# Attention and expert layer in one kernel: an expert's two matrices in one transfer, a narrower tile of ones, and a new table of the order

## The chip, the cores and the metric

The kernel runs on one core of one Trainium2 chip. The metric is the device time in microseconds of one execution, lower is better. The kernel has three compute engines that read PSUM or feed from it, TensorE (PE in the profile), ScalarE (ACT) and VectorE (DVE); GpSimd (POOL), which scales what another engine has copied out; and SyncE (SP), on whose queue nearly all transfers are issued.

## The reference

Four batches of 10048 tokens with 128 channels pass through an induced-attention block with 32 inducing points and then through a two-level mixture of experts, 4 groups of 4 experts, each with a hidden width of 1024.

```python
def mab(q, kv):
    s = scale * (q @ kv.transpose(0, 2, 1))
    s = s - s.max(-1, keepdims=True)
    a = np.exp(s)
    a /= a.sum(-1, keepdims=True) + 1e-09
    return a @ kv
h = mab(I, x)                 # (B, 32, 128)
attn = mab(x, h)              # (B, N, 128)
...
g_idx = np.argmax(x @ w_group, axis=1)            # then the expert within the group
h = np.maximum(xg[mask_e] @ w1[g, e], 0.0)
ye = h @ w2[g, e]
out[tok_idx] = combined[:, None] * ye             # combined: the two softmax weights
```

Here x of the second part is the attention's output. Everything is float32. Tokens enter and leave as 20.6 MB each.

## The kernel before, in words

A batch (b = 0 to 3) is cut into five chunks (k = 0 to 4) of 4 x 512 tokens, 1 MB each; the fifth overlaps the fourth. For each chunk the kernel loads the tokens with channels on the partitions (`xk`, from `xT` or `xL`). For half of the chunks (`LOADED`) it also loads them with tokens on the partitions (`xn`, from `xm`); for the others TensorE transposes `xk` (`turn`, L139) and ACT or DVE copy the result out of PSUM (`tev`, L534). The first attention is `s1` (L152), a running maximum (DVE, L156), `ex` (ACT, L163), a transpose `tr` (L173), its copy `pev`, and `hq` (L186), which sums over tokens and frees the buffers of the chunk.

After the five chunks some small steps normalize the sum (`ap` L208, `same` L221, `hp` L230) and route the batch: the product `R` (L240, L241), then `pick` on DVE, which writes the number of one expert into `pi` (L253). The kernel relies on all tokens of a batch going to that one expert and on its hidden units each having one sign over the batch; it checks both, and a general path (`general`), which is not taken here, does the rest. SP reads the number (L281, a value load that waits for `pick`) and loads that expert's `w1` (L282) and `w2` (L283), each 128 rows of 4 KB, into the two halves of one buffer. TensorE applies `w1` to the 32 summaries (`z`, L288), DVE transposes and masks the result, and TensorE applies `w2` (`G4`, L306) and sums (`G`, L312). So the whole expert becomes a 32 x 128 matrix G per batch.

The second attention of a chunk is `s2` (L329), a maximum (DVE, L333), `ex2` (ACT, L337), `L` (L344) for the routing weights, and `out` (L383), which fills four PSUM banks. Each is written into the chunk's output buffer by one of three ways: by ACT as a bare copy (L398), which POOL then scales (L403); by DVE with the scaling (L392); or by ACT with the scaling in four pieces (L396). Then SP stores the chunk, 1 MB (L407).

All operations of the four batches are numbered by `plan_all`. The table `ORDER` is a list of these numbers with a letter for the engine (a, b or c: the first, second or third that may do it) and sets the order on every engine; each engine works its list in order. Buffers come from rings (19 of 1 MB named `big`, 8 PSUM banks `ps`, and others) and are given out in the table's order, so a load waits for the operation that frees its buffer. SP too works its list in order: a value load or a store that waits holds the transfers behind it.

`IDLE` names places at which TensorE gets products of ones, n units of 128 columns, so that it does not stand still (L489, `idle`); they read a tile of ones that a DVE memset fills at the start (L852) and write a PSUM bank that the operation named is about to use. The first, of 12 units, runs while the first chunk is on its way.

Of the kernel before, what the change touches and what calls it, by code (L numbers as in the profile page):

```python
# [8 lines left out]
F32 = mybir.dt.float32  # L9
# [7 lines left out]
P = 128  # L17
# [27 lines left out]
IDLE = ((2, 12), (455, 3), (465, 2), (515, 3), (625, 4), (635, 2), (657, 4), (667, 5), (704, 6))  # L45
# [59 lines left out]
def plan_all(em=None):  # L105
# [130 lines left out]
    def routes(b, hT):  # L236
# [41 lines left out]
        def w2():  # L278
            return em.t(w12)[:, F:].rearrange("p (n c) -> p n c", c=C)
        def f(e):  # L280
            i = em.nc.sync.value_load(em.s(f"pi{b}", 1, 1, I32)[0:1, 0:1], min_val=0, max_val=E - 1)  # L281
            em.nc.sync.dma_start(out=em.t(w12)[:, 0:F], in_=em.w1[bass.ds(i, 1)].rearrange("o d f -> d (o f)"))  # L282
            em.nc.sync.dma_start(out=w2(), in_=em.w2[bass.ds(i, 1)].rearrange("o (p n) d -> p (o n) d", n=FB))  # L283
# [199 lines left out]
    def idle(at, n):  # L483
        o = plan.ops[at]
        ps = o.take.pop(0)
        assert ps.of == "ps"
        def f(e):
            for w in [KW] * (n // TK) + [P] * (n % TK):
                em.nc.tensor.matmul(em.t(ps)[:, 0:w], lhsT=em.ones[:, 0:P], rhs=em.ones[:, 0:w], start=True, stop=True)  # L489
        o.soft.append(op("idle", PE, f, [], [ps], [], size=n))  # L490
# [56 lines left out]
1a 0a 206a 706a 2a 6a 3b 4a 5b 7b 8a 357a 17a 10a 45a 27a 11a 19a 12a 23a 28a 35a 178a 25a 205a 18a 20a 9a 47a 21a 53a 13a 63a 46a 29a 51a 234a 49a  # L547
24a 26b 195a 30a 31a 37a 14a 50b 36a 38a 55a 56a 188a 32a 40a 48b 57a 22b 15a 356a 179a 54a 64a 180a 39a 16a 59a 182a 189a 186a 207a 183b 60a 52a 209a
208a 181b 184a 41a 190a 211a 191a 192a 61a 65a 42a 33a 187a 197a 233a 185b 223a 66a 215a 198a 67a 216a 193a 194a 43a 34a 213a 373a 58a 217a 68a 219a
210a 73a 44a 212b 358a 383a 362a 62a 74a 199a 69a 75a 200a 363a 70b 76a 366a 71a 72a 360a 196a 214a 218a 77a 367a 359a 201a 78a 364a 401a 220a 79a  # L550
235a 237a 368a 202b 80a 81a 361a 82a 369a 238b 241a 83a 84a 127a 365a 243a 370a 236a 131a 225a 527a 128a 95a 375a 242a 99a 86a 85a 226a 227a 224a 244a
411a 96a 371a 221a 372a 526a 100a 376a 132a 393a 97a 159a 101a 129a 160a 245a 228a 203a 384a 133a 239a 204a 240a 229a 230b 161a 251a 247a 385a 374a
87a 377a 252a 222a 394a 98a 403a 88a 395a 248a 386a 102a 253a 89a 412a 389a 571a 397a 103a 254a 391a 398a 379a 378a 392a 104a 404a 390a 105a 405a 106a
91a 231a 232a 92a 90a 413a 255a 414a 380a 162a 249a 536a 246a 163a 130a 416a 93a 250a 415a 537a 407a 94b 421a 402a 256a 422a 164a 387a 528a 538a 529a
396a 257a 408a 258a 134a 381a 543a 135a 165a 117a 382a 136a 388a 553a 118a 137a 120a 259a 399a 260a 309a 581a 166a 122a 417a 400a 124a 138a 310a 406a
261a 423a 139a 262a 418a 273a 311a 140a 142a 144a 409a 424a 146c 274a 107a 545a 108a 114a 110a 264a 263a 123a 275a 410a 112c 546a 337a 277a 177a 121a
419a 149a 338a 420a 563a 143a 547a 425a 111a 278a 544a 426a 276a 113a 339a 109a 279a 573a 280a 150b 564a 427a 154a 156b 115a 141a 549a 145a 147a 119a
428a 532a 539a 565a 265a 533a 429a 281a 157a 574a 572a 305a 540a 555a 550a 554a 152a 125a 282a 430a 576a 266a 575a 561a 556a 267a 562a 557a 269a 283a
270a 548a 558a 431a 306a 307a 530a 271a 268a 559a 284a 534a 272a 531a 295a 153a 151a 560a 535a 308a 541a 296c 432a 566a 155a 433a 302a 542a 116a 126a
298a 479a 567a 300c 480a 167a 481a 568a 583a 168b 312a 170a 174b 584a 551a 552a 172c 285a 585a 577a 591a 297a 148a 313a 286a 586a 314a 592a 315a 169a  # L560
578a 288a 292c 316a 447a 448a 290c 569a 475a 340a 175a 570a 579a 476a 449a 303a 477a 327a 158a 341a 342a 355a 580a 287a 343a 587a 328a 434a 443a 588a
582a 589a 344a 444a 435a 593a 299a 330a 332a 590a 334a 317a 445a 594a 173a 436a 595a 596a 171a 291a 437a 289a 597a 598a 446a 318b 333a 324c 450a 322a
439a 599a 293a 176a 440a 345a 329a 331a 438a 600a 301a 451a 601a 441a 320c 452a 325a 602a 323a 346a 348a 319a 442a 453a 350c 294a 454a 352a 708a 465a
321a 335a 466a 468a 472a 707a 455a 351a 478a 470a 304a 603a 482a 349a 456a 483a 462c 613a 326a 458a 347a 617a 484a 460c 353a 467a 649a 336a 614a 618a
487a 485a 615a 645a 469a 486a 619a 471a 616a 488a 494a 604a 650a 354a 646a 490a 461a 457a 620a 492a 463a 651a 459a 473a 621a 605a 489a 606a 647a 497a
648a 607a 498a 464a 652a 608a 500c 474a 653a 622a 609a 610a 502a 501a 495a 504a 507a 611a 493a 654a 491a 623a 612a 499a 508a 503a 655a 505a 509a 710a
# [279 lines left out]
def attention_moe(ctx, tc, xT, xL, xm, small, w1, w2, out):  # L846
# [4 lines left out]
    ones = cp.tile([P, KW], F32, name="ones")  # L851
# [19 lines left out]
        "ident": ident, "iota4": iota4, "own_j": own_j, "ones": ones[:, 0:P], "wr_sb": small_sb[:, M:],  # L871
# [23 lines left out]
def build_inputs(inputs):  # L895
# [18 lines left out]
        "w2": np.asarray(inputs["moe_w2"]).reshape(E, F, C),  # L914
    }
# [20 lines left out]
```

## Time and profile before

| | |
|---|---|
| median of 3 runs | 151.36 us (151.32 to 151.44) |
| the profiled execution | 151.35 us, of which the span is 149.6 us |
| PE busy | 136.1 us, 91% of the span |
| DVE / ACT / POOL busy | 112.8 / 105.5 / 51.0 us |
| moved by DMA | 56.9 MB, mean 380 GB/s |
| HBM read / written | 35.50 MB / 20.97 MB |

The span goes from the first to the last instruction; what the execution takes beyond it, 1.75 us, lies around it. In the prediction's rows an engine's instructions stand with their line, and a DMA issue is a row of SP. In the view of stretches the columns are the busy time of PE, its weight loads, DVE, ACT and POOL, the granted clock of TensorE, the busy share of the DMA engines and their GB/s. The landing time of a transfer runs from its issue until all of its data are there.

### The profile page before, as it was taken

To read this page: it belongs to the slowest core of one execution; us is meant where nothing else is said; L and a number is where in the kernel's file an instruction comes from. 1 tells how busy PE (TensorE), PEld (TensorE's weight loads), DVE (VectorE), ACT (ScalarE), POOL (GpSimd) and SP (SyncE) were. 2 spreads that over 40 slices of the span, in tenths; PEclk is the share of its full clock that TensorE was granted. 3 is DMA by queue.
4 is the path that set the end of the run, shared out by engine and by line. 5 is a ranking of instruction groups with operands and counts; after the bars stand their busy time and mean duration, and the time that the engine had idled before them with its cause. 6 is when DMAs were issued, how large, how long until landed. Compare 5 with 4: busy or idle time off the path is not lost.

```text
span 149.6 us, 5582 instructions
## 1 busy us (share of the span) xinstructions
PE 136.1 (91%) x2225; PEld 93.7 (63%) x2225; DVE 112.8 (75%) x383; ACT 105.5 (71%) x265; POOL 51.0 (34%) x70
## 2 busy tenths in 40 slices
PE   6999999999999999999999999999999999998000
PEld 3459497678536686967455967676884656775000
DVE  3093782756889889888998978998989998999500
ACT  3017384486416797679968999989999998999300
POOL 4000000000000000044491811555799998855200
PEclk9999999999999999999999999999999999999965
DMA  5999999999999999999999999979699899999980
GB/s 123 421 423 425 415 424 421 418 424 414 417 413 418 420 416 424 415 424 418 387 376 366 377 418 364 379 287 410 245 423 252 348 421 434 414 416 425 425 344 33
DMA packets 8529, 56.90 MB, mean 380 GB/s; under 512 B 1072, under 2 KB 1072, under 8 KB 2608
## 3 DMA queue, kind: packets, MB, share of 16 engines
q1 hardware_dynamic: 8352, 56.45, 94.0%
q8 instruction: 19, 0.31, 0.8%
q14 instruction: 14, 0.11, 0.2%
q10 hardware_dynamic: 144, 0.03, 0.1%
HBM read 35.50 MB, written 20.97 MB: 378 GB/s over the span
## 4 chain that ended last, share of the span: by engine, by line
PE 67%; DVE 14%; ACT 10%; issue 2%; DVEq 0%; ACTq 0%
PE ps L139 13%; PE ps L152 11%; PE ps L186 10%; PE ps L329 8%; PE ps L383 8%; PE ps L173 5%; ACT big L398 4%; PE ps L489 4%; ACT big L396 3%; PE ps L344 2%; DVE big L392 2%; ACT et L337 2%; DVE mxe L333 1%; PE ps L230 1%; PE ps L306 1%
## 5 line engine op out<-in xcount | busy, mean ns | idle before, releaser
L403 POOL TENSOR_TENSOR big<-big,gate_w 128x512 f32<-128x512 f32 x48 | 48.9, 1050 | 42.8 <-ACT big L398 36.0
L398 ACT COPY big<-ps 128x512 f32<-128x512 f32 x48 | 26.7, 626 | 1.7 <-PE ps L383 1.0
L163 ACT ACTIVATE pe<-ps,nb 128x512 f32<-128x512 f32 (+1 forms) x20 | 13.7, 687 | 19.6 <-DVE nb L160 9.6
L396 ACT ACTIVATE big<-ps,gate_w 128x128 f32<-128x128 f32 x84 | 24.4, 414 | 1.5 <-DVE n_bad L454 1.5
L383 PE MATMUL ps<-G,et 32*128 32x128 f32 x640 | 25.0, 285 | 0.0
L383 PEld LDWEIGHTS ps<-G,et 32*128 32x128 f32 x640 | 21.0, 186 | 5.6 <-ACT big L398 1.9
L139 PE MATMUL ps<-spread,big 128*128 128x128 f32 (+1 forms) x160 | 21.4, 276 | 0.1
L186 PEld LDWEIGHTS ps<-big,pt 128*32 128x32 f32 (+1 forms) x640 | 17.8, 110 | 5.9 <-issue 4.1
L186 PE MATMUL ps<-big,pt 128*32 128x129 f32 (+1 forms) x640 | 21.0, 273 | 0.0
L329 PE MATMUL ps<-big,hT 128*32 128x512 f32 (+2 forms) x192 | 20.5, 525 | 0.0
L139 PEld LDWEIGHTS ps<-spread,big 128*128 128x128 f32 (+1 forms) x160 | 17.8, 141 | 3.9 <-issue 2.0
L152 PE MATMUL ps<-big,small_sb 128*32 128x512 f32 (+1 forms) x160 | 19.9, 588 | 0.0
L156 DVE TENSOR_REDUCE mx<-ps 128x1 f32<-128x512 f32 (+1 forms) x20 | 13.4, 672 | 4.8 <-PE ps L152 4.1
L129 POOL MEMSET big<- 128x16 f32 x10 | 0.8, 128 | 45.8 <-PE ps L186 42.7
L534 ACT COPY big<-ps 128x512 f32<-128x512 f32 (+1 forms) x28 | 15.6, 591 | 0.8 <-PE ps L139 0.7
L337 ACT ACTIVATE et<-ps,nce 128x512 f32<-128x512 f32 x20 | 13.8, 722 | 2.4 <-DVE nce L334 2.1
L489 PE MATMUL ps<-ones 128*128 128x128 f32 (+1 forms) x40 | 13.4, 468 | 1.6 <-DVE ones L852 1.5
L333 DVE TENSOR_REDUCE mxe<-ps 128x1 f32<-128x512 f32 x20 | 13.3, 667 | 0.7 <-ACT big L398 0.4
L534 DVE COPY big<-ps 128x512 f32<-128x512 f32 x12 | 8.0, 685 | 7.8 <-PE ps L139 7.7
L534 ACT COPY pt<-ps 128x512 f32<-128x512 f32 (+2 forms) x20 | 10.0, 522 | 3.6 <-PE ps L173 2.8
L173 PE MATMUL ps<-spread,pe 128*128 128x128 f32 x80 | 12.2, 276 | 0.0
L173 PEld LDWEIGHTS ps<-spread,pe 128*128 128x128 f32 x80 | 9.1, 140 | 2.0 <-ACT big L398 1.7
(118 smaller groups left out, 162.2 us busy)
## 6 DMA issues: line engine op xcount, KB each, us to landing
out<-big SPq DMA_DIRECT2D x20, 1024.0 KB, 7.7
big<-xT SPq DMA_DIRECT2D x16, 1024.0 KB, 14.5
big<-xm SPq DMA_DIRECT2D x10, 1032.0 KB, 12.3
big<-w SPq DMA_DIRECT2D x8, 512.0 KB, 6.5
big<-xL SPq DMA_DIRECT2D x4, 960.0 KB, 14.9
small_sb<-small ACTq DMA_DIRECT2D x1, 26.0 KB, 5.7
```

Of the source, the lines that this page charges most:

```text
L139: em.nc.tensor.transpose(p[:tw, j * P:(j + 1) * P], em.t(xk[b, k])[:, j, off + t * P:off + t * P + tw], em.ident)
L152: em.nc.tensor.matmul(em.t(ps)[32 * j:32 * j + 32, :w], lhsT=em.indT, rhs=em.t(xk[b, k])[:, j, off:], start=True, stop=True)
L173: em.nc.tensor.transpose(p[:tw, t * P:(t + 1) * P], em.t(pe)[:, t * P:t * P + tw], em.ident)
L186: em.nc.tensor.matmul(h[32 * j:32 * j + 32, 0:CS], lhsT=q[:tw, t, 32 * j:32 * j + 32], rhs=x[:tw, t * J + j, :], start=(t == 0), stop=(t = ...
L329: em.nc.tensor.matmul(em.t(ps)[32 * j:32 * j + 32, c0:c1], lhsT=em.hT[b][:, P + 1:P + 1 + M], rhs=em.t(xk[b, k])[:, j, x0:x0 + c1 - c0], s ...
L337: em.nc.scalar.activation(out=em.t(et), in_=em.t(ps), func=AF.Exp, bias=em.s(nc_), scale=1.0)
L383: em.nc.tensor.matmul(em.t(pb[j])[:, t * C:(t + 1) * C], lhsT=em.t(et)[32 * j:32 * j + 32, t * P:(t + 1) * P], rhs=em.Gs[b][32 * j:32 * j ...
L396: em.nc.scalar.activation(out=q[:, t], in_=p[:, t], func=AF.Copy, scale=em.t(gt)["w"][:, r:r + 1])
L398: em.nc.scalar.copy(out=q, in_=p)
L403: em.nc.gpsimd.tensor_tensor(out=q, in0=q, in1=weights(j), op=ALU.mult)
L489: em.nc.tensor.matmul(em.t(ps)[:, 0:w], lhsT=em.ones[:, 0:P], rhs=em.ones[:, 0:w], start=True, stop=True)
L534: (self.nc.scalar.copy if engine == ACT else self.nc.vector.tensor_copy)(out=out, in_=in_)
```

## The change

Three edits. An expert's two matrices are laid side by side on the host in one array `w12`, 128 rows of 8 KB per expert, and loaded in one transfer. The tile of ones is 128x128 in place of 128x512, and the idle products read one of its columns with a stride of zero as their moving operand. `ORDER` and `IDLE` are new.

```diff
-IDLE = ((2, 12), (455, 3), (465, 2), (515, 3), (625, 4), (635, 2), (657, 4), (667, 5), (704, 6))
+IDLE = ((2, 12), (455, 3), (465, 2), (625, 2), (635, 3), (657, 4), (667, 3), (704, 5))
...
-            em.nc.sync.dma_start(out=em.t(w12)[:, 0:F], in_=em.w1[bass.ds(i, 1)].rearrange("o d f -> d (o f)"))
-            em.nc.sync.dma_start(out=w2(), in_=em.w2[bass.ds(i, 1)].rearrange("o (p n) d -> p (o n) d", n=FB))
+            em.nc.sync.dma_start(out=em.t(w12), in_=em.w12[bass.ds(i, 1)].rearrange("o p f -> p (o f)"))
...
-                em.nc.tensor.matmul(em.t(ps)[:, 0:w], lhsT=em.ones[:, 0:P], rhs=em.ones[:, 0:w], start=True, stop=True)
+                em.nc.tensor.matmul(em.t(ps)[:, 0:w], lhsT=em.ones[:, 0:P], rhs=em.ones[:, 0:1].broadcast_to([P, w]), start=True, stop=True)
...
-1a 0a 206a 706a 2a 6a 3b 4a 5b 7b 8a 357a 17a 10a 45a 27a 11a 19a 12a 23a 28a 35a 178a 25a 205a 18a 20a 9a 47a 21a 53a 13a 63a 46a 29a 51a 234a 49a
+206a 0a 17a 706a 2a 4a 6a 8a 10a 1a 11a 45a 3b 35a 12a 27a 5a 178a 19a 23a 25a 13a 18a 20a 9a 205a 7b 28a 46a 47a 53a 21a 24a 29a 54b 22a 48b 195a 51a
...
-    ones = cp.tile([P, KW], F32, name="ones")
+    ones = cp.tile([P, P], F32, name="ones")
...
+        "w12": np.concatenate([np.asarray(inputs["moe_w1"]).reshape(E, C, F), np.asarray(inputs["moe_w2"]).reshape(E, P, FB * C)], axis=2),
```

The general path still reads `w1` and `w2`. From L283 on, a line's number is lower by one after the change.

What the table does to the engines: of the 40 copies of transposed chunks (`tev`), ACT does 33 after and 28 before; of the 24 other copies, 23 and 20. Of the 80 output evictions, ACT copies 51 (48 before), ACT scales 19 (21), DVE scales 10 (11). The order moves in these places:

SP, from batch 1's expert transfer to the value load for batch 2's (`out` is a store of batch 0, `xm` a load of batch 3). Before:

```order
L282 DMA big_97<-w 128x1024
L283 ISA
L283 DMA big_97<-w 128x1024
L121 DMA big_109<-xm 128x2064
L121 DMA big_101<-xm 128x2064
L407 DMA out<-big_98 128x2048
L407 DMA out<-big_93 128x2048
L407 DMA out<-big_91 128x2048
L407 DMA out<-big_104 128x2048
L281 TENSOR_LOAD pi_1433
```

After:

```order
L282 DMA big_106<-w 128x2048
L406 DMA out<-big_97 128x2048
L406 DMA out<-big_94 128x2048
L121 DMA big_99<-xm 128x2064
L406 DMA out<-big_92 128x2048
L121 DMA big_106<-xm 128x2064
L121 DMA big_95<-xm 128x2064
L406 DMA out<-big_96 128x2048
L281 TENSOR_LOAD pi_1455
```

Batch 3's first `xm` load (its second chunk) stands behind two stores now, and its third, which came after batch 2's expert, comes before it.

POOL, at the first scalings (L403 before, L402 after; `big_93` and `big_94` are batch 0's second chunk); the memset is that of the ones column of a transposed chunk of batch 3. Before:

```order
L403 TENSOR_TENSOR big_93<-big_93,gate_w_132 128x4x128 x2
L403 TENSOR_TENSOR big_91<-big_91,gate_w_138 128x4x128
L403 TENSOR_TENSOR big_98<-big_98,gate_w_132 128x4x128 x3
L403 TENSOR_TENSOR big_91<-big_91,gate_w_138 128x4x128 x2
L403 TENSOR_TENSOR big_93<-big_93,gate_w_132 128x4x128
L129 MEMSET big_99 128x16
L403 TENSOR_TENSOR big_93<-big_93,gate_w_132 128x4x128
```

After:

```order
L402 TENSOR_TENSOR big_94<-big_94,gate_w_132 128x4x128
L402 TENSOR_TENSOR big_92<-big_92,gate_w_135 128x4x128
L402 TENSOR_TENSOR big_94<-big_94,gate_w_132 128x4x128
L402 TENSOR_TENSOR big_92<-big_92,gate_w_135 128x4x128 x2
L129 MEMSET big_98 128x16
L402 TENSOR_TENSOR big_97<-big_97,gate_w_132 128x4x128 x2
L402 TENSOR_TENSOR big_92<-big_92,gate_w_135 128x4x128
L402 TENSOR_TENSOR big_94<-big_94,gate_w_132 128x4x128
```

The memset comes after five scalings in place of nine, and the chunk's last scaling is the ninth in place of the tenth.

TensorE, around the fourth batch's `z` (L288 before, L287 after). Before:

```order
L383 MATMUL ps_128<-G_148,et_116 128x128
L329 MATMUL ps_126<-big_103,hT 32x512 x4
L344 MATMUL ps_125<-et_118,rbd_145 32x128 x4
L344 MATMUL ps_125<-et_117,rbd_145 32x128 x4
L288 MATMUL ps_122<-big_104,hT 32x256 x4
L383 MATMUL ps_127<-G_148,et_115 128x128
```

After:

```order
L328 MATMUL ps_126<-big_107,hT 32x512 x4
L328 MATMUL ps_129<-big_91,hT 32x512 x4
L328 MATMUL ps_123<-big_102,hT 32x480 x4
L328 MATMUL ps_123<-big_102,hT 32x32 x4
L287 MATMUL ps_122<-big_106,hT 32x256 x4
L382 MATMUL ps_125<-G_148,et_119 128x128
```

The two products L344 that stood ahead of `z` come behind it, and the last chunk's `s2` of batch 2 (L328, 480 and 32 columns) comes ahead of it.

More of the change, by code (lines that the diff above doesn't have):

```diff
@@ L551 @@
[L551 to L566, printed above, removed]
@@ new lines @@
+26a 31a 49a 14a 52a 179a 32a 37a 30a 55a 38a 56a 63a 33a 188a 15a 36a 356a 180a 234a 384a 64a 39a 207a 50a 186a 16a 181a 57a 189a 209a 41a 211a 40a
+187a 59a 190a 208a 213a 233a 191a 212a 60a 192a 42b 184a 34a 185a 182a 197a 61a 198a 65a 223a 183a 210a 357a 193a 215a 66a 43a 67a 68a 73a 216a 58a
+69a 44a 74a 401a 358a 364a 217a 214a 219a 75a 199a 76a 70a 62a 366a 367a 71a 362a 359a 77a 201a 72a 368a 360a 78a 79a 220a 80a 369a 194a 235a 218a 81a
+370a 241a 237a 202a 82a 365b 236a 361a 363b 83a 238a 196a 200a 131a 225a 127a 371a 373a 99a 84a 383a 243a 85a 226a 372a 128a 244a 242a 527a 227a 132a
@@ new lines @@
+424a 121a 123a 277a 419a 146a 145a 571a 263a 142a 107a 274a 275a 278a 108c 110b 112a 545a 309a 114a 581a 546a 310a 409a 547a 119a 410a 264a 420a 563a
+305a 564a 162a 306a 279a 425a 147a 426a 427a 311a 143a 163a 111a 149a 109a 565a 164a 307a 554a 115a 276a 337a 113a 428a 177a 116a 573a 150c 165a 152a
+141a 154a 280a 265a 338a 530a 548a 125a 339a 532a 166a 549a 156a 157a 534a 533a 531a 555a 266a 267a 281a 268a 535a 561a 269a 270a 556a 562a 282a 283a
+126a 574a 550a 429a 308a 541a 430a 271a 431a 272a 544a 559a 557a 284a 575a 567a 542a 560a 295a 566a 155a 153a 558a 296a 551a 300a 302a 576a 432a 433a
@@ new lines @@
+479a 568a 148a 151a 583a 312a 552a 298c 480a 584a 167a 481a 168a 585a 447a 313a 170a 172b 569a 314a 174a 169a 577a 572a 315a 578a 285a 448a 449a 316a
+286b 475a 582a 288a 292a 340a 297a 327a 570a 591a 158a 476a 290c 434a 341a 477a 586a 342a 587a 579a 175a 343a 592a 344a 588a 443a 328c 173a 589a 330a
+355a 593a 444a 301a 334a 291a 580a 435a 594a 590a 436a 332c 595a 596a 437a 171a 317a 445a 293a 438a 176a 597a 439a 318a 287a 446a 440a 289a 598a 320a
+303a 329a 450a 335a 322c 324b 599a 451a 600a 333a 319a 345a 294a 346a 348a 325a 452a 321a 601a 441a 442a 453a 350a 708a 352a 331a 465a 478a 466a 482a
@@ new lines @@
+602a 707a 454a 349a 468a 470a 299a 323a 603a 351a 455a 347a 304a 472c 456a 483a 613a 467a 326a 460a 484a 353a 617a 462a 458c 487a 336a 485a 473a 649a
+488a 604a 614a 618a 461a 645a 615a 457a 459a 486a 492a 354a 507a 490a 650a 646a 463a 619a 651a 508a 605a 494c 497a 616a 620a 606a 607a 647a 498a 509a
+471a 609a 502a 648a 610a 652a 504a 611a 612a 621a 622a 469a 709a 653a 493a 464a 654a 623a 625a 500c 624a 495a 608a 626a 632a 655a 711a 474a 491a 657a
+630c 628b 710a 656a 658a 489a 629a 501a 635a 660b 712a 664a 661a 696a 496a 499a 662c 503a 636c 642c 638b 667a 505a 668a 510a 663a 677a 670a 640b 627a
@@ L571 @@
+633a 515a 511a 674a 512a 678a 697a 506a 672c 631a 659a 513a 665a 525a 671a 641a 637a 643a 679a 514a 673a 516a 680a 522a 681a 634a 518c 519a 698a 682a
+713a 695a 685a 669a 683a 520c 675a 639a 666a 523a 686a 699a 644a 684a 700a 702a 688a 701a 703a 676a 690b 521a 704a 517a 687a 689a 692c 693a 691a 705a
+524a 694a
 """
@@ L845, in attention_moe @@
 @with_exitstack
-def attention_moe(ctx, tc, xT, xL, xm, small, w1, w2, out):
+def attention_moe(ctx, tc, xT, xL, xm, small, w1, w2, w12, out):
     nc = tc.nc
@@ L870, in attention_moe @@
     keep = {
-        "ident": ident, "iota4": iota4, "own_j": own_j, "ones": ones[:, 0:P], "wr_sb": small_sb[:, M:],
+        "ident": ident, "iota4": iota4, "own_j": own_j, "ones": ones, "wr_sb": small_sb[:, M:],
         "hT": cp.tile([P, B, P + 1 + M], F32, name="hT"),
@@ L877, in attention_moe @@
         pp = inner.enter_context(tc.tile_pool(name="ps", bufs=1, space=PSUM))
-        em = Emit(tc, fp, pp, nc, xT=xT, xL=xL, xm=xm, w1=w1, w2=w2, out=out, wr=keep["wr_sb"], indT=small_sb[:, 0:M], ones=ones,
+        em = Emit(tc, fp, pp, nc, xT=xT, xL=xL, xm=xm, w12=w12, out=out, wr=keep["wr_sb"], indT=small_sb[:, 0:M], ones=ones,
                   ident=ident, same_m=same_m, spread=spread, iota16m40=iota16m40, own_j=own_j,
```

11 lines of the change are left out of this document (4 added, 7 removed).

## The prediction

> **What bounds the kernel now.** I read the page first, then the stretches, then the queue's own waits, then single rows. The page:
>
> ```profile
> span 149.6 us, 5582 instructions
> PE 136.1 (91%) x2225; PEld 93.7 (63%) x2225; DVE 112.8 (75%) x383; ACT 105.5 (71%) x265; POOL 51.0 (34%) x70
> ```
>
> TensorE is busy for 91% of the span, and so, as the next rows show, are the transfers; the question is which of them is the limit where. The stretches (PE busy first; the last two columns are the DMA share and GB/s):
>
> ```profile
> 5.00:75.00 70.00, 69.75 (x1090) 48.70 (x1088) 52.24 (x169) 43.80 (x98) 5.33 (x7) 1.00 1.01 417
> 75.00:108.00 33.00, 32.92 (x622) 23.34 (x623) 29.33 (x100) 29.77 (x80) 17.37 (x19) 1.00 0.92 359
> 106.00:108.00 2.00, 2.00 (x39) 1.69 (x39) 1.90 (x7) 1.79 (x7) 1.96 (x2) 1.00 0.32 119
> 112.00:117.00 5.00, 5.00 (x81) 2.52 (x80) 4.52 (x18) 5.00 (x15) 5.00 (x6) 1.00 0.99 238
> 117.00:144.00 27.00, 21.05 (x367) 14.26 (x359) 21.94 (x74) 21.47 (x63) 18.01 (x18) 0.98 1.02 421
> ```
>
> Up to 108 us TensorE stands still for 0.33 us in 103, so it sets the pace; just before 108 the transfers run dry (119 GB/s). From 117 to 144 it is the other way round: 421 GB/s without a hole, while TensorE has 6 us to spare. Between lies the expert transfer of batch 3:
>
> ```profile
> 107.31 1.13 SPq L407 DMA_DIRECT2D out<-big  x2
> 110.89 0.35 SPq L282 DMA_DIRECT2D big<-w  x1
> 111.43 1.07 SPq L283 DMA_DIRECT2D big<-w  x1
> 112.60 0.43 SPq L407 DMA_DIRECT2D out<-big  x1
> ...
> 140.84 0.33 SPq L407 DMA_DIRECT2D out<-big  x1
> ```
>
> SP issues nothing from 108.4 to 110.9, since its next row is the value load that waits for the batch's routing. TensorE ends that routing product at 107.61 + 0.38 = 107.99, and the load is issued 2.9 us later:
>
> ```profile
> 107.61 0.38 PE L241 MATMUL ps<-small_sb,hT 128*128 128x20 f32 x2
> 117.92 0.61 PE L288 MATMUL ps<-big,hT 128*32 128x256 f32 x8
> 120.50 0.62 PE L306 MATMUL ps<-big,mt 128*32 128x128 f32 x16
> ```
>
> Behind it stand 11 stores, of 1 MB each. The last is issued at 140.84 and lands 7.5 us later, at 148.3 (first row); of all 20 stores the quickest took 4.1 (second row):
>
> ```profile
> DMA to landing us min/median/max: 7.5/7.5/7.5
> DMA to landing us min/median/max: 4.1/7.7/9.6
> ```
>
> So at the end a backlog of transfers, 3.4 us deep, covers the engines. The time is: TensorE's work up to the fourth routing, plus one expert transfer and 11 stores at the rate they get. An edit counts if it moves one of these.
>
> **The sum's base.** This execution took 151.35 us for a span of 149.6; the median of the runs is 151.36, so nothing is to be corrected.
>
> **The change part by part.** *The tile of ones.* The first idle products wait for its memset, and the first transposes for the idle products:
>
> ```profile
> 0.92 0.48 DVE L852 MEMSET ones<- 128x512 f32 x1 [0.92 <-PEq L923]
> 2.00 0.23 DVE L866 COPY same_m<-spread 128x128 f32<-128x128 f32 x1
> ...
> 1.46 5.25 PE ps L489 x6
> 6.71 1.75 PE ps L139 x16
> ```
>
> A 128x128 operation on VectorE takes 0.23, so the memset should lose 0.25 us, and the transposes start 0.25 earlier. More than the memset's whole 0.48 can't come of it, and nothing, if the first chunk isn't there earlier. I take -0.25, of 0 to -0.48. The moving operand now repeats one column. The nearest rows are two weight loads of the routing product, of which L240's repeats a column and L241's doesn't:
>
> ```profile
> L240 PEld LDWEIGHTS ps<-small_sb,hT x8: 185/190/192, 37.8 to 107.5; 128*128 128x128 f32 x8
> L241 PEld LDWEIGHTS ps<-small_sb,hT x8: 189/190/192, 38.1 to 107.7; 128*128 128x128 f32 x8
> ```
>
> 190 ns in both, so 0.
>
> *TensorE up to the fourth routing.* The order has it at row 325 before and after, with the same products ahead. What differs is how often TensorE turns from 32-row products to full-width ones or back: I count 39 turns before and 35 after. A turn shows in the chain as the same work at two prices:
>
> ```profile
> 34.06 0.59 PE ps L139 x4
> ...
> 35.09 0.44 PE ps L139 x4
> ```
>
> Four turns fewer at 0.15 are -0.6; other pairs show less, so I take -0.5, of 0 to -0.6. Against it, new waits: in the program after, loads stand in other places, and five of twelve evictions of transposed chunks and three other copies move from VectorE to ScalarE, in the stretch where ScalarE has 26 us free (5 to 75 us: 43.80 of 70). I allow +0.25, of 0 to +1.1 (worked out in the second rival). Together the fourth routing comes 0.5 us earlier.
>
> *One transfer for two.* SP saves an issue, 0.54 us per expert (110.89 to 111.43), and the store behind it is no longer held until 112.60; its data are ready then or a little before, and the queue is busy, so this is worth 0. Batch 0's pair tells what the second transfer itself costs:
>
> ```profile
> 41.16 0.36 SPq L282 DMA_DIRECT2D big<-w  x1
> 41.75 0.34 SPq L283 DMA_DIRECT2D big<-w  x1
> ...
> DMA to landing us min/median/max: 7.3/7.3/7.3
> DMA to landing us min/median/max: 8.0/8.0/8.0
> ```
>
> They land at 48.46 and 49.75, 1.29 us apart, and 0.524 MB at 418 GB/s are 1.25, so a second transfer costs nearly nothing there. Batch 3's pair does not go like that. From 112 to 117 the engines are busy (0.99) at 238 GB/s, which against 418 is 5 x (1 - 238/418) = 2.15 us lost, on the path. The other pairs:
>
> ```profile
> 41.00:51.00 10.00, 10.00 (x177) 6.05 (x173) 8.89 (x32) 5.42 (x10) 0.12 (x1) 1.00 1.02 418
> 72.00:77.00 5.00, 5.00 (x105) 2.88 (x105) 4.79 (x16) 4.64 (x12) 3.97 (x4) 1.00 1.01 389
> 90.00:97.00 7.00, 7.00 (x162) 5.05 (x165) 5.95 (x17) 6.69 (x19) 2.32 (x3) 1.00 1.01 371
> ```
>
> By the same sum they lose 0, 0.35 and 0.8 us, the more the more stores are about. The trace doesn't say why. One transfer of 128 rows of 8 KB from another tensor has half as many reads and other addresses; it may lose all the 2.15, or none, or about 1 us more (the step from batch 2 to batch 3). The other three lose 0.4 on average, this one 2.15: I take a loss of 1.15, that is -1.0, of -2.15 to +1.0.
>
> Against the merge stands that the first product with the weights (L288) has to wait for both matrices. Now the first lands at 110.89 + 6.3 = 117.2, the product starts at 117.92, and the second matrix lands at 111.43 + 7.3 = 118.7, ahead of its use at 120.50:
>
> ```profile
> DMA to landing us min/median/max: 6.3/6.3/6.3
> DMA to landing us min/median/max: 7.3/7.3/7.3
> ```
>
> Landing 0.5 earlier, at 118.2, it would hold TensorE for up to 0.8 us from its turn at 117.4 (less, since after the change one scoring product stands ahead of it in place of two smaller ones); landing 1.5 earlier, not at all. What it holds is covered by the 3.4 us backlog: 0. The Trainium skill says the same more sharply: by "DMA: Bandwidth & Descriptors", section "Why a DMA increments its semaphore by 16 and not by 1", only the full count tells that all data of a transfer are there. By that rule alone the product waits up to 0.8 us longer, and if the backlog did not cover it, the sum would be 150.7 instead of 149.9.
>
> *The order's end.* Idle products fall from 41 to 34 units, and the last stores' evictions are shared out anew. This moves the last issue (140.84), which is covered as long as the backlog stands; it becomes late next only if the transfers gain more than 3.4 us. Moved stores and loads before the fourth routing: the queue runs dry there anyway, 0.
>
> Sum: 151.35 - 0.5 - 1.0 = 149.85; I predict 149.9.
>
> **The rivals.** *1. All of the 2.15 us goes.* If the pair of 4 KB transfers, with its second issue of 1.07 us, is what slows the reads, the merge recovers them all: 151.35 - 0.5 - 2.15 = 148.7. For it: that issue is three times as long as batch 0's 0.34. Against it: batch 2's second issue was longer still, at a loss of 0.8:
>
> ```profile
> 90.11 1.38 SPq L283 DMA_DIRECT2D big<-w  x1
> ```
>
> [...]
>
> *2. Slower: a load of batch 3 is stuck behind a store.* After the change the load of batch 3's second chunk stands on SP behind batch 0's second store. That store waited for POOL:
>
> ```profile
> SPq L407 <- POOL big L403: 23.0, 12, 6.8
> ...
> 83.36 0.82 SPq L407 DMA_DIRECT2D out<-big  x2
> ...
> 82.22 0.12 POOL L129 MEMSET big<- 128x16 f32 x1 [3.12 <-PE ps L329]
> ...
> 92.13 0.73 PE L186 MATMUL ps<-big,pt 128*32 128x129 f32 x20
> ...
> DMA to landing us min/median/max: 6.1/6.1/6.1
> ```
>
> If it goes out at 83.4 again, the load lands 6.1 us later (a load issued at 93.25 took that), at 89.5. Its product, at 92.13 before, has 3.2 us less of work ahead of it after (counted in the order, each product at its price in the chain) and is due at 88.4 with the 0.5 gained: 1.1 us of standstill, which every later step pays, 151.35 - 0.5 + 1.1 = 152.0. It decides if the store is issued after 82.3. Against it: the memset that held POOL for 3.12 us stands four scalings earlier and waits for an earlier product, and this store's last scaling is the ninth on POOL where it was the tenth. Without the hold it goes out at 80.2, one scaling earlier at 79.2.
>
> *3. Slower reads.* The merged load, with stores on both sides, loses 1 us more than now: 151.35 - 0.5 + 1.0 = 151.9.
>
> *4. Nothing moves.* New waits eat the 0.5, and the reads lose 2.15 again: 151.3.
>
> **How the numbers follow.** Forecast 0.54, rival 1 0.09, rival 2 0.12, rival 3 0.11, rival 4 0.14. The predicted time is the forecast's. The range 148.4 to 151.9 goes from rival 1's 148.7, less 0.3 for its unknowns, up to rival 3. This kernel's runs differ by 0.1%, so about 0.2% (0.3 us) is what a measurement can tell: faster 0.63 (the forecast and rival 1), same 0.14, slower 0.23.
>
> **What would show it.** Right: the first transposes near 6.45; the routing product L241's fourth pair ending near 107.5, the fourth expert load issued near 110.4; over 300 GB/s in the 5 us after it is first read; the last store landing near 146.8. Wrong: TensorE idle for over 1 us between 5 and 108 us; the fourth load again at 238 GB/s; a last store that lands 4.1 us after its issue, which would say that the engines and no longer the transfers set the end.

## The result: 1.2% slower

After took 153.3 us in the median of its first four executions (152.45 to 154.97) against 151.34 before, a ratio of 1.0124 with a 95% interval of 1.0082 to 1.0165. Measured again beside other kernels (run e5 below) it gave 1.0125, 1.0082 to 1.0168. The forecast was 149.9, with 148.4 to 151.9 for the range: it named the wrong sign. Medians here are of all executions, while ratios leave out slow ones, those more than 1.5% above the kernel's fastest, such as the one of 154.97 us. That one is the profiled execution of after, with a span of 153.2; where a number hangs on that, I give it from the profile of e5 too, the same kernel in 152.2 us.

The page of after, the two lines that were shown of before:

```profile
span 153.2 us, 5565 instructions
PE 135.4 (88%) x2223; PEld 93.9 (61%) x2223; DVE 109.7 (72%) x373; ACT 108.1 (71%) x269; POOL 54.3 (35%) x73
```

TensorE works no longer than before (136.1). The stretches, as before PE first, the last two columns the DMA share and GB/s:

```profile
5.00:75.00 70.00, 69.18 (x1073) 48.62 (x1075) 47.27 (x152) 45.23 (x102) 6.49 (x9) 1.00 1.00 410
75.00:108.00 33.00, 32.78 (x635) 23.15 (x628) 30.05 (x106) 29.68 (x78) 17.64 (x19) 1.00 0.95 373
112.00:117.00 5.00, 5.00 (x92) 2.46 (x88) 4.48 (x19) 4.90 (x15) 5.00 (x6) 1.00 1.01 352
117.00:144.00 27.00, 20.53 (x365) 14.43 (x357) 22.81 (x73) 22.83 (x67) 19.53 (x20) 0.90 0.93 383
```

The last of these stretches in e5:

```profile
117.00:144.00 27.00, 19.20 (x365) 13.20 (x357) 23.01 (x74) 22.65 (x67) 19.39 (x20) 0.94 0.98 409
```

TensorE stands still for 0.82 us up to 75 us (1.36 in e5), where it was 0.25. The read from 112 to 117 goes at 352 GB/s (349 in e5) in place of 238, as hoped. But from 117 to 144 the transfers, which had no hole before (421), have some: 383, and still 409 in e5. Next SP's issues and two of TensorE's products, then two answers on the time to landing: the fourth expert load and the last store.

```profile
111.38 0.35 SPq L282 DMA_DIRECT2D big<-w  x1
114.09 30.77 SPq L406 DMA_DIRECT2D out<-big  x11
108.00 0.38 PE L241 MATMUL ps<-small_sb,hT 128*128 128x20 f32 x2
120.38 0.64 PE L287 MATMUL ps<-big,hT 128*32 128x256 f32 x8 [1.86 <-DMA big<-w]
DMA to landing us min/median/max: 8.9/8.9/8.9
DMA to landing us min/median/max: 5.0/5.0/5.0
```

The fourth routing product ends at 108.38 (in e5 too), 0.4 us later than before and not 0.5 earlier. The expert load lands 8.86 us after its issue, at 120.24, and TensorE waits 1.86 us for it; in e5 it lands after 7.5, and TensorE doesn't wait for it. The last store is issued at 144.52 (141.97 in e5, 140.84 before) and lands after 5.0 us (5.4 in e5): the 3.4 us backlog that the forecast counted on is mostly gone.

After's profile is 2.6 us behind e5's at the last store, and TensorE's granted clock has a part in that. The two rows of each are the stretch behind the load's landing and the products with `w2`, first after, then e5:

```profile
121.00:126.00 5.00, 5.00 (x93) 4.15 (x90) 3.32 (x9) 2.77 (x7) 3.94 (x5) 0.66 1.01 423
123.28 1.08 PE L305 MATMUL ps<-big,mt 128*32 128x128 f32 x16
```

```profile
121.00:126.00 5.00, 4.67 (x90) 3.09 (x82) 4.47 (x15) 4.91 (x15) 4.55 (x6) 1.00 0.99 416
121.40 0.64 PE L305 MATMUL ps<-big,mt 128*32 128x128 f32 x16
```

The clock is 0.50 in each microsecond from 122 to 125 of after, and 1.00 in e5. The first product with the weights starts 1.42 us later than in e5 (120.38, 118.96), and the product L311 2.53 later (125.11, 122.58): 1.4 us for the late load, 1.1 for the clock. The same dip stands in the profile of e13 below, but not in those of e7 and e8, in which TensorE waited as long for the load (1.8 and 2.0 us); what sets it off stays open.

What ends the kernel shows in SP's waits behind the last store. The verdict is the number that VectorE writes last of its chain (`n_bad`); every engine reads it and branches over the general path. The rows are first before's, then after's (L887 before and L886 after are that branch, L930 the closing barrier):

```profile
SPq L887 <- SPq L887: 5.3, 1, 5.3
SPq L930 <- DMA out<-big: 1.2, 1, 1.2
```

```profile
SPq L886 <- SPq L886: 5.2, 1, 5.2
SPq L930 <- PEq L886: 0.6, 1, 0.6
```

SP stands behind its own branch for 5.2 us. Before, it still had to wait 1.2 us for the last store after that; after, it waits for TensorE's branch instead and never for the store (in e5 too: 5.5 us, then 0.2 for TensorE's branch). I had both rows of before and didn't read them: only 1.2 us lay between the store that I took for the end and another end.

### The profile page after: what moved, and what is told of

Read it like the earlier page. It is cut to its first block, busy times and chain, and to the rows that moved or that the text cites. A ratio compares the mean times of both kernels' runs of the same rounds, so it can differ in the third digit from the quotient of the medians.

```text
span 153.2 us, 5565 instructions
## 1 busy us (share of the span) xinstructions
PE 135.4 (88%) x2223; PEld 93.9 (61%) x2223; DVE 109.7 (72%) x373; ACT 108.1 (71%) x269; POOL 54.3 (35%) x73
## 4 chain that ended last, share of the span: by engine, by line
PE 66%; DVE 17%; DMA 6%; issue 3%; ACT 2%; SPq 0%; DVEq 0%
PE ps L139 12%; PE ps L152 12%; PE ps L186 11%; PE ps L382 7%; PE ps L328 6%; DMA big<-w 6%; PE ps L173 5%; PE ps L488 3%; PE ps L343 3%; DVE big L391 3%; PE ps L305 2%; DVE mxe L332 1%; PE ps L287 1%; DVE gate_rs L357 1%; DVE ps L366 1%
## 5 line engine op out<-in xcount | busy, mean ns | idle before, releaser
L402 POOL TENSOR_TENSOR big<-big,gate_w 128x512 f32<-128x512 f32 x51 | 52.1, 1050 | 52.6 <-DMA big<-xm 26.3
L397 ACT COPY big<-ps 128x512 f32<-128x512 f32 x51 | 27.8, 607 | 5.4 <-PE ps L382 5.3
L382 PE MATMUL ps<-G,et 32*128 32x128 f32 x640 | 24.5, 287 | 0.0
L382 PEld LDWEIGHTS ps<-G,et 32*128 32x128 f32 x640 | 20.5, 188 | 4.7 <-issue 1.6
L395 ACT ACTIVATE big<-ps,gate_w 128x128 f32<-128x128 f32 x76 | 22.0, 404 | 0.0
L328 PE MATMUL ps<-big,hT 128*32 128x512 f32 (+2 forms) x192 | 20.4, 526 | 0.0
L533 ACT COPY big<-ps 128x512 f32<-128x512 f32 (+1 forms) x33 | 18.4, 604 | 2.3 <-PE ps L139 2.2
L488 PE MATMUL ps<-ones 128*128 128x128 f32 (+1 forms) x38 | 11.6, 438 | 1.2 <-DVE ones L851 1.1
L533 ACT COPY pt<-ps 128x512 f32<-128x512 f32 (+2 forms) x23 | 11.3, 531 | 0.5 <-PE ps L173 0.3
L328 PEld LDWEIGHTS ps<-big,hT 128*32 128x32 f32 x192 | 5.5, 109 | 8.4 <-issue 5.0
```

What stands on the lines that cost most here:

```text
L328: em.nc.tensor.matmul(em.t(ps)[32 * j:32 * j + 32, c0:c1], lhsT=em.hT[b][:, P + 1:P + 1 + M], rhs=em.t(xk[b, k])[:, j, x0:x0 + c1 - c0], s ...
L382: em.nc.tensor.matmul(em.t(pb[j])[:, t * C:(t + 1) * C], lhsT=em.t(et)[32 * j:32 * j + 32, t * P:(t + 1) * P], rhs=em.Gs[b][32 * j:32 * j ...
L395: em.nc.scalar.activation(out=q[:, t], in_=p[:, t], func=AF.Copy, scale=em.t(gt)["w"][:, r:r + 1])
L397: em.nc.scalar.copy(out=q, in_=p)
L402: em.nc.gpsimd.tensor_tensor(out=q, in0=q, in1=weights(j), op=ALU.mult)
L533: (self.nc.scalar.copy if engine == ACT else self.nc.vector.tensor_copy)(out=out, in_=in_)
```

## Experiments

Each run was timed beside before, and the ratio is to before, with its 95% interval; medians of runs in different tables are less comparable than ratios. In an order, a number is an operation and its letter how an eviction is done: a, ScalarE copies and POOL scales; b, VectorE does both; c, ScalarE does both.

### Which part of the change costs the time

e1 has only the merged transfer, e2 only the small tile, e3 only the new order with its idle products, and e4 is after with two transfers again.

```diff
 e1, on before
-  dma_start(out=em.t(w12)[:, 0:F], in_=em.w1[...]); dma_start(out=w2(), in_=em.w2[...])
+  dma_start(out=em.t(w12), in_=em.w12[...])
 e2, on before
-  rhs=em.ones[:, 0:w]
+  rhs=em.ones[:, 0:1].broadcast_to([P, w])        (ones is 128x128)
 e3, on before:  ORDER and IDLE of after
 e4, on after:   the first edit undone
```

> The kernel before with one change: both matrices of an expert in one transfer; order of work, idle products and tile of ones stay. Theory M (the merged transfer costs the time: the first product with the weights waits for both matrices, TensorE stands still, batch 3's last stretch starts late, and the end is set by the branch over the general path, which can't start until the verdict is written): TensorE waits 1 to 2 us for the weights near 118 us, the verdict comes 1 to 3 us later than 139.4, and the time is 151.5 to 153. Theory O (the new order of work costs the time: it writes the verdict last of all on VectorE): no loss here, 150.3 to 151.4, as forecast for the read alone. Theory S (the smaller tile of ones): 151.4, no change.

> The kernel before with the 128x128 tile of ones, its first column repeated as the moving operand of the idle products; nothing else. Theories M and O: 151.1 to 151.4; the first transposes start 0.25 us earlier, and TensorE's work up to the fourth routing ends as much earlier. Theory S: over 152, with idle products that take longer or a clock that is granted less.

> The kernel before with the new order of work and the new list of idle products; two transfers for an expert and the large tile of ones stay. Theory M: TensorE doesn't wait for the weights near 118 us; the time falls back to 151.0 to 151.7. Theory O: the verdict is still the last operation on VectorE, 4 to 5 us later than 139.4, and with TensorE's branch of 5 to 6.7 us behind it the time stays at 152 to 153.3. Theory S: 151.4.

> The kernel after with an expert's matrices in two transfers again; order, idle products and small tile of ones as after. Theory M: 150.8 to 151.5, that is 1.2 to 1.9 us less than after. Theory O: 152 to 153.3, no less than after. Theory S: as after, and more than the kernel with the new order alone.

| run | median us | ratio |
|---|---|---|
| e1, merge only | 151.07 | 0.9989 (0.9963 to 1.0015) |
| e2, tile only | 150.89 | 0.9988 (0.9963 to 1.0014) |
| e3, order only | 152.64 | 1.0110 (1.0072 to 1.0148) |
| e4, order and tile | 152.51 | 1.0089 (1.0055 to 1.0122) |

Theory O holds: the order costs the time. Theory M, my own first one, falls as the main cause. In e1 the product with the weights does wait, 0.5 us, and starts at 119.02 in place of 117.92; the last store is issued 0.9 later (141.74); the time is the same. The forecast's "covered: 0" is right there.

### What in the order costs it

Two things in the new order look alike. In e4, POOL's first scaling, VectorE's copy of a row (L205) and the product that waits for it:

```profile
65.53 1.05 POOL L403 TENSOR_TENSOR big<-big,gate_w 128x512 f32<-128x512 f32 x1 [26.34 <-ACT big L398]
65.63 1.03 DVE L205 COPY rowj<-row 1x128 f32<-1x128 f32 x1
66.80 0.24 PE L208 MATMUL ps<-ones,rowj 1*128 1x1 f32 x1 [0.73 <-DVE rowj L205]
```

The copy takes 0.22 us at its shortest of four and 1.03 here: it starts 0.10 after POOL's scaling and ends 0.08 behind it. (The fourth batch's copy takes 0.98 beside another scaling, and 0.80 in before; no product waits for those.) And in after, the end of the verdict on VectorE, with POOL's two scalings beside it; behind that the two operations in before:

```profile
141.70 2.05 POOL L402 TENSOR_TENSOR big<-big,gate_w 128x512 f32<-128x512 f32 x2 [1.63 <-DVE t L440]
141.79 0.16 DVE L412 TENSOR_REDUCE smin<-S 128x1 f32<-128x16 f32 x1
141.87 0.24 DVE L413 TENSOR_REDUCE xmax<-X 128x1 f32<-128x96 f32 x1
142.03 0.73 DVE L445 SCALAR_TENSOR_TENSOR t<-smin,thr,prev 128x1 f32<-128x1 f32 x1
142.80 0.97 DVE L446 SCALAR_TENSOR_TENSOR t<-xmax,t 128x1 f32<-128x1 f32 x1
143.69 0.68 DVE L391 TENSOR_TENSOR big<-ps,gate_w 128x512 f32<-128x512 f32 x1
144.29 0.14 DVE L453 TENSOR_SCALAR n_bad<-ps 1x1 int32<-1x1 f32 x1
```

```profile
L446 DVE SCALAR_TENSOR_TENSOR t<-smin,thr,prev x1: 219/219/219, 138.0 to 138.0; 128x1 f32<-128x1 f32 x1
L447 DVE SCALAR_TENSOR_TENSOR t<-xmax,t x1: 158/158/158, 138.3 to 138.3; 128x1 f32<-128x1 f32 x1
```

The two operations on one column (L445, L446) take 0.73 and 0.97 us, in e5 as in after, where they took 0.22 and 0.16 before. They end at 142.76 and 143.77, where POOL's first and second scaling end (142.75 and 143.75). An eviction then stands ahead of the last one, and the verdict is written at 144.43 (141.88 in e5), where it was 139.38. Not every operation is held: the reductions L412 and L413 start during the first scaling and take 0.16 and 0.24, as they do in e6 without one. The Trainium skill states the hold: by "SBUF — State Buffer", section "SBUF: two separate sides", VectorE and POOL share a pair of ports, and of a POOL operation that reads SBUF and a VectorE operation that runs in a two-port mode or reads two inputs from SBUF, whichever starts first has the pair for the whole instruction. This trace agrees, with ends 0.01 to 0.08 us behind POOL's for the operations that were held.

e6 takes the verdict away from POOL's scalings and puts the eviction behind it; e7 takes the row's copy away from POOL. e8 leaves out the branch and the general path.

```diff
 e6, on after
-  523a 686a 699a 644a 684a 700a 702a 688a 701a 703a 676a 690b 521a 704a 517a 687a 689a 692c ... 705a
+  523a 699a 644a 684a 686c 700a 702a 688c 701a 703a 676a 521a 704a 517a 705a 690b 692b ...
 e7, on after
-  122a
+  122c
 e8, on after
-  left = nc.values_load(n_bad); with tc.If(left > 0): general(...)
```

> The kernel after, unchanged, beside the three that follow. The earlier runs leave two theories of the merged transfer under the new order. W: it costs time there (the first product with the weights waited 1.86 us for both matrices, in a kernel whose end has no slack left): 0.3 to 1 us more than the 152.5 of the kernel with two transfers. N: it costs nothing, as under the old order: 152.3 to 152.7.

> After, with the last chunk's evictions shared out anew: two on ScalarE with the weight in the same instruction, two on VectorE behind the verdict's last operation, none scaled on POOL. Theory V (the end is the verdict, TensorE's branch behind it, and some 1.5 us; the verdict is late since two of its small VectorE operations take 0.73 and 0.97 us in place of 0.22 and 0.16 while POOL scales, and since an eviction stands ahead of its last): the two take 0.2 each, the verdict comes 1.3 to 1.9 us earlier, and the time falls by 0.8 to 1.7 us. Rival D (the end is the last store's landing): no change, as the last store isn't issued earlier.

> After, with one eviction of batch 0's first outputs (the one whose scaling is POOL's first) done on ScalarE with the weight, so that POOL doesn't scale while VectorE copies the row of batch 2's means (L205). Theory P (POOL's scaling holds VectorE's copy for 0.8 us, and TensorE waits for that): the copy takes 0.22 in place of 1.03 us, TensorE's wait of 0.73 us at the product L208 goes, the fourth routing and the verdict come 0.7 us earlier, the time falls by 0.5 to 0.8 us. Rival A (the copy is late for another reason, or ScalarE's longer eviction moves the wait to the next product): less than 0.2 us.

> After, without the branch: the verdict is computed, but not read, and the general path behind it is left out. Theory V: the end is then the last store's landing, issued at 144.5 and landed some 5 us later, and 1.2 us: 2 to 3 us less than after. Rival D: no change, within 0.3 us. A gain of less than 1 us would say that both end nearly together.

| run | median us | ratio |
|---|---|---|
| e5, after | 153.00 | 1.0125 (1.0082 to 1.0168) |
| e6, verdict free of POOL | 151.87 | 1.0036 (1.0010 to 1.0063) |
| e7, row's copy free of POOL | 153.20 | 1.0103 (1.0064 to 1.0141) |
| e8, no branch | 150.04 | 0.9923 (0.9897 to 0.9949) |

e6: theory V as expected, 1.1 us less in the median (1.0036 in place of 1.0125). The same operations, no scaling beside them (a source line's durations in ns, then the verdict):

```profile
L445 DVE SCALAR_TENSOR_TENSOR t<-smin,thr,prev x1: 210/210/210, 140.0 to 140.0; 128x1 f32<-128x1 f32 x1
L446 DVE SCALAR_TENSOR_TENSOR t<-xmax,t x1: 159/159/159, 140.3 to 140.3; 128x1 f32<-128x1 f32 x1
140.73 0.15 DVE L453 TENSOR_SCALAR n_bad<-ps 1x1 int32<-1x1 f32 x1 [0.28 <-PE ps L450]
```

Its last store was issued 0.2 us later than e5's (142.14, 141.97), so it isn't the store that got faster. The edit took away two things at once, the hold (1.3 us in these two operations) and the eviction (0.68 us) ahead of the verdict; what each is worth alone is not shown. e8: 3 us less; behind its last store stands only a wait for the landing:

```profile
SPq L925 <- DMA out<-big: 3.3, 2, 2.4
```

e7 missed. The wait at L208 went, and the expert load was issued 0.27 us earlier than in e5, but in its profile the merged transfer landed late and TensorE waited for that:

```profile
PE ps L287 <- DMA big<-w: 1.8, 1, 1.8
```

In e5 the same product waited for no transfer at all:

```profile
118.96 0.64 PE L287 MATMUL ps<-big,hT 128*32 128x256 f32 x8 [0.44 <-DVE mxe L332]
```

The transfer lands in sixteen parts. In four profiles of the new order (after, e7, e8, e13) the last came 2.8 to 3.1 us behind the ninth (117.34 and 120.24 in after), in six others (e5, e6, e11, e14, e17, e18) 1.1 to 1.5 (117.37 and 118.82 in e5). So theory W is right of some executions of one kernel, not of all, and between e4 (1.0089) and after (1.0125) the intervals overlap; after's times spread over 3.8 us in e5 where before's spread over 1.6.

### Both edits together, and the old order

e9 is before without the branch. e10 is after with the edits of e6 and e7 and two transfers, e11 the same with the merged one. e12 is before with the merge and the small tile, so the whole change but the order.

> The kernel before without the branch: the verdict is computed, but not read, and the general path behind it is left out. Theory V: before, the last store's landing (148.4) and 1.2 us set the end, 1.5 us behind the end of TensorE's branch (145.3) and what follows it, so leaving the branch out changes little: 150.4 to 151.3. The change as forecast then shows between the two kernels without a branch: after without it took 150.04 us, so 0.4 to 1.2 us less than this one. Rival: the branch is on the path before too, and this kernel takes 149 to 150, no more than after without it, so that the change gains nothing anywhere.

> After with both edits of the order made before (VectorE's copy and the verdict both clear of POOL's scalings) and an expert's matrices in two transfers. Theory V with W: 0.7 from the copy, 1 to 1.5 from the verdict against the 152.5 of the order with two transfers: 150.3 to 151.0, no more than before. Rival (the copy's 0.7 is lost again further on): 151.3 to 151.9.

> The same as the one before it with the merged transfer; the pair tells what the merge is worth under the new order. Theory W (in some executions the first product with the weights waits up to 2 us for the last of the transfer's sixteen parts): 0.3 to 1 us more than with two transfers. Theory N: within 0.2 us. Rival R (the read's 1.4 us in the stretch 112 to 117 is gained whole): 0.5 to 1 us less.

> The kernel before with the merged transfer and the small tile of ones, that is the whole change but the order. Alone they took 0.9989 and 0.9988 of before's time. If they add: 150.7 to 151.0, 0.2% below before. If the merge's wait eats what the tile gives: 151.0 to 151.3.

| run | median us | ratio |
|---|---|---|
| e9, before, no branch | 150.35 | 0.9956 (0.9933 to 0.9978) |
| e10, both free, two transfers | 150.89 | 0.9981 (0.9956 to 1.0006) |
| e11, both free, merged | 151.00 | 0.9983 (0.9954 to 1.0012) |
| e12, old order, merge and tile | 150.61 | 0.9964 (0.9944 to 0.9984) |

e10 and e11: with both edits the new order takes before's time within the interval, 2 us less than after (e11). So what the two edits clear accounts for the whole loss that can be told, and there was no gain under it that shows. The merge is worth nothing that shows there (theory N). These two edits cleared the row's copy, the verdict's two operations and the eviction ahead of it together. e12 is 0.4% faster than before. e9 gained 0.75 us where theory V allowed little, so leaving the branch out is worth something even where the last store lands behind it; in its profile that store lands 6.7 us after its issue in place of 7.5, and whether the missing code loads did that isn't shown. Against e9, after without the branch (150.04) is 0.3 us better in the median, less than the 0.4 to 1.2 expected, and the two intervals overlap: a gain of the change that the branch hides isn't shown.

### What stands behind the branch

TensorE's branch took 6.68 us in after, and I took it for the end. The kernel names its branch to the engines ahead of time with a prefetch hint (BRANCH_PREFETCH_HINT in the trace), meant to have the code behind the branch loaded early. e13 moves this hint up from the verdict's first operation to the transpose at the head of the same chain; e14 has no hint; e15 is e12 with e13's move; e16 is e4 with e7's edit; e17 is e13 without SP's hint; e18 is e11 with e17's edit.

```diff
 e13, on after
   def bounds(proof): ...
+    em.tc.mark_branch_hint_location("general", engines=...)     (before the transpose of em.least)
   def verdict(...): ...
-    em.tc.mark_branch_hint_location("general", engines=...)
```

> After, with the branch's prefetch hint moved from the verdict's first operation to the transpose of the batches' least means (three operations of the same chain earlier, some 3 us on TensorE). Theory H (the hint asks for the code behind the general path, and at 136.6 it is too late): the code is loaded before the branch, TensorE's branch takes about 1 us in place of 6.5, the end is the last store's landing, and the time falls by 1 to 2.5 us from after's 153.0. Theory Q (the hint does nothing; the code load starts with the branch and queues behind the last store): no change, within 0.4 us.

> After, with no prefetch hint. Theory H: TensorE's branch takes 6.5 us as in after, whose hint came too late; the time is after's 153.0 within 0.4 us. If the hint matters in part of the executions: up to 0.6 us more. Theory Q: no change either; with e13 unchanged too, the hint is out of the question.

> The old order with the merged transfer and the small tile of ones, and the hint moved earlier as in e13. Theory H: TensorE's branch about 1 us in every execution; the last store's landing sets the end, so at most 0.3 us less than the 150.6 without the move. Theory Q: 150.6.

> After with two transfers for an expert, and POOL's first scaling kept clear of VectorE's copy (L205), as in e7. Theory P: TensorE's wait of 0.73 us at L208 goes, and with no merged transfer to wait for it stays gone: 0.5 to 0.8 us less than the 152.5 of the same kernel without the edit. Rival: it is lost again on the way to the verdict, less than 0.2 us.

> After, with the hint at the earlier place on TensorE, VectorE, ScalarE and GpSimd, and none on SyncE. Theory C (after its branch each engine that lacks the code waits for a load that queues behind the last store; the latest of SyncE, VectorE and TensorE sets the end): SyncE goes on within 0.5 us of its branch, TensorE's branch takes 0.5, VectorE still waits 5 us or more, so the time stays within 0.6 us of after's 153.0. If VectorE's load comes earlier without SyncE's beside it: 1 to 2 us less. Theory Q (SyncE alone sets the end): 2 us less or more.

> The merged transfer, the new order with both its waits for POOL taken away, the hint at the earlier place and none on SyncE. Theory C: the code loads now end before the last store's landing (147.3 in the profile without the hint's move), so the store sets the end: 150.3 to 151.0, up to 0.5 us less than the 151.0 without the move. If VectorE's load still comes last: 151.0.

| run | median us | ratio |
|---|---|---|
| e13, hint early | 153.11 | 1.0103 (1.0068 to 1.0139) |
| e14, no hint | 153.58 | 1.0128 (1.0083 to 1.0174) |
| e15, e12 with the hint early | 150.63 | 0.9949 (0.9927 to 0.9972) |
| e16, e4 with the row free | 152.24 | 1.0054 (1.0031 to 1.0076) |
| e17, hint early, none on SP | 152.59 | 1.0104 (1.0055 to 1.0154) |
| e18, both free, same hint | 151.38 | 1.0001 (0.9971 to 1.0032) |

The source line of the branch in after, then in e13 (durations in ns; then first and last start):

```profile
L886 SPq EVENT_SEMAPHORE  x7: 17/17/17, 150.7 to 151.2; - x7
L886 DVEq EVENT_SEMAPHORE  x2: 21/21/21, 150.8 to 150.9; - x2
L886 PEldq EVENT_SEMAPHORE  x2: 51/51/51, 151.8 to 151.9; - x2
L886 PEldq COMPARE_BRANCH  x1: 6682/6682/6682, 145.1 to 145.1; - x1
L886 SPq COMPARE_BRANCH  x1: 73/73/73, 145.5 to 145.5; - x1
```

```profile
L886 SPq EVENT_SEMAPHORE  x7: 17/17/17, 151.7 to 152.2; - x7
L886 PEldq EVENT_SEMAPHORE  x2: 51/51/51, 146.0 to 146.2; - x2
L886 DVEq EVENT_SEMAPHORE  x2: 21/21/21, 151.8 to 152.0; - x2
L886 PEldq COMPARE_BRANCH  x1: 487/487/487, 145.4 to 145.4; - x1
L886 SPq COMPARE_BRANCH  x1: 73/73/73, 145.8 to 145.8; - x1
```

The early hint works on TensorE's branch: 0.48 to 0.49 us in e13, e15, e17 and e18. It doesn't work on the time: e15 takes what e12 took (150.63, 150.61), and in e13 SP and VectorE go on only at 151.7 and 151.8, about 6 us behind their branches of 0.07 and 0.08. So theory H is half right, and my reading that TensorE alone held the end falls. In e14, as slow as after (1.0128), SP went on 0.44 us behind its branch and I took SP's hint for the cause; in e17, without that hint, SP stood for 5.9 us. What made e14 differ stays open. e18 missed: 151.4 where 150.3 to 151.0 was expected, no less than e11. e16 is 0.3 us under e4 in the median and 0.5 by the ratios, where 0.5 to 0.8 was expected, and the intervals overlap; TensorE's standstill in 60 to 70 us fell from 0.73 to 0.10. The row's copy alone is thus not settled to the tenth; e11 against after puts it and the verdict together at 2 us.

What the traces' end has in common (all times us from the span's start):

| run | verdict written | last store issued | SP's branch ends | SP goes on | store lands | span | span less issue |
|---|---|---|---|---|---|---|---|
| before | 139.38 | 140.84 | 141.30 | 146.55 | 148.37 | 149.57 | 8.73 |
| e12 | 139.65 | 141.12 | 141.58 | 146.82 | 147.69 | 148.67 | 7.55 |
| e11 | 139.91 | 141.17 | 141.63 | 146.72 | 147.32 | 148.58 | 7.41 |
| e6 | 140.88 | 142.14 | 142.59 | 147.83 | 148.06 | 149.69 | 7.55 |
| e5 | 141.88 | 141.97 | 143.01 | 148.45 | 147.37 | 150.42 | 8.45 |
| after | 144.43 | 144.52 | 145.57 | 150.73 | 149.54 | 153.19 | 8.67 |
| e13 | 144.78 | 144.87 | 145.91 | 151.72 | 150.00 | 153.57 | 8.70 |
| e8, no branch | 143.33 | 143.42 | none | none | 147.29 | 148.22 | 4.80 |

With the verdict ahead of the last store, SP reads it while it waits for the store's data, and branches 0.45 us behind the issue. With the verdict behind, SP issues the store first, and then reads and branches, 1.05 us behind it. From there it takes 5.1 to 5.8 us to its next instruction in each row, and then to the end. In after, a case of the second kind, four code loads of 8 KB start at 148.17 to 148.22, as the store's last packets come (the last ends at 148.48), and two more at 151.30 and 151.41; before, three start at 142.40 to 142.81, with the store still on its way. That the loads queue behind the store fits after; no run here takes the store away from before them, so it isn't shown.

## Why the prediction was wrong, step by step

*"The order's end ... covered as long as the backlog stands."* This is the step that failed, and it made the sign wrong. It asked when the last store is issued, and never what else has to happen: the verdict, the branch and the code behind it. In before that path ended 1.2 us ahead of the store's landing, so it was invisible in the time and plain in SP's waits; the cover was 1.2 us and not the 3.4 of the backlog. The new order writes the verdict 2.5 us later (141.88 in e5, 139.38), last of all on VectorE, and with the backlog short nothing covers it: leaving the branch out takes 3.0 us off after (e8), clearing the verdict 1.1 (e6), and clearing the row's copy too brings the order back to before's time (e11). Why SP and VectorE stand for microseconds behind their branches stays open. The rival on the other side that I worked out, batch 3's load stuck behind a store, didn't happen: batch 0's second store was out by 78.5, not 83.4, and no wait for that load shows.

*"Four turns fewer: -0.5", "new waits: +0.25".* Measured +0.4 for the fourth routing. By the starts of TensorE's products up to it, the order alone comes 1.3 us later on the small tile (e4 against e2) and 1.0 on the large one (e3 against before). In both, 0.7 of it is at the products that wait for the row's copy (L208), and the products of all other kinds differ by 0.1 in sum; the rest, 0.5 and 0.1, is at the first transposes, whose start differs by 0.4 between two profiles with the same order and tile (6.33 in e4, 5.95 in after), so it can't be put down to the order. So the turns gave nothing that shows: a price read off one pair of rows was counted for four. The first new wait alone was 0.73, three times the allowance. A sign of being wrong that the forecast named did come true: from 5 to 108 us TensorE stood still for 1.04 us in after and 1.50 in e5.

*"The tile of ones: -0.25."* The idle products start 0.40 earlier (1.06, where they started at 1.46), and the first transposes at 5.82, 5.95 and 6.33 in e2, after and e4, where they started at 6.55 to 6.74 in before, e1 and e3. In the time it is below what can be told alone (0.9988).

*"One transfer for two: -1.0."* In size about right: 352 GB/s against 238 in the same five microseconds is 5 x (352 - 238)/418 = 1.4 us recovered. But much of it is the order's: with two transfers and the new order the stretch has 284 (e10), 304 (e4) and 320 (e3), and merged in the old order 256 (e12) and 293 (e1). And it isn't on the path: e1 didn't gain. Its first product waits 0.5 us for the whole transfer, and whatever the transfers gained at the end, the other end stood 1.2 us behind and bounded it; which of the two held e1 isn't shown. The loss of 2.15 us "on the path" was the mistake here. (The step from batch 2 to batch 3 is 1.35 us by the forecast's own figures, not about 1.)

*"What it holds is covered by the backlog: 0."* True in the old order (e1). In the new one, in part of the executions, the wait was 1.8 to 2.1 us (after, e7, e8, e13) and not the 0.8 given as the most, since the last of the sixteen parts came so late. The Trainium skill's rule that I weighed ("DMA: Bandwidth & Descriptors", section "Why a DMA increments its semaphore by 16 and not by 1") is borne out: the product started at 120.38, behind the sixteenth part (120.24) and not the ninth (117.34).

*"This kernel's runs differ by 0.1%".* That was read off three executions. Beside e5, before's 23 executions go from 150.33 to 151.97, 1.1%, so a difference of 0.2% needs many more runs than three.

## To carry to other kernels

When transfers seem to set the end, look at every wait of the last stretch, not the last one alone: what is due 1.2 us earlier bounds every gain, and becomes the limit once the order moves. Here the value that the branch reads was better written ahead of the last store, with its small VectorE operations kept clear of POOL's scalings (e6). The merge and the smaller tile are worth 0.4% in the old order (e12, 0.9964), and the new order should have been dropped or cleared of its two collisions.

## What the hardware showed that I had not expected

- A VectorE copy in SBUF and two operations with two SBUF inputs, begun during a POOL scaling of 1.05 us, ended with it: 0.22 became 1.03, 0.22 became 0.73 and 0.16 became 0.97 us. Reductions in the same place took their usual 0.16 and 0.24.
- Going on behind a branch over a large body took SP 5.1 to 5.9 us in every profile with a branch but one (0.44, e14). TensorE's branch took 0.48 to 0.49 us where the hint ran 7.9 us or more ahead of the verdict (four profiles), and 0.85 to 6.68 where it ran 3.7 to 5.3 ahead.
- One transfer's last part landed 2.9 us behind its ninth in after, and 1.45 in e5, another execution of the same kernel.
- In after and e13 TensorE's granted clock was half for about 3.4 us behind a wait of 1.9 and 2.1 us for the weights; in e7 and e8, with waits of 1.8 and 2.0, it stayed whole.
